# Attention and FFN with a Fourier stage: the scaled rows and the folds of the first two batches move from VectorE to GpSimd

## The chip, the core and the metric

The kernel runs on one core of a Trainium2 chip. Five engines of that core work side by side, each through its own list of instructions in a fixed order: TensorE (matmuls and transposes, PE in the profile), VectorE (DVE), ScalarE (ACT), GpSimd (POOL) and SyncE (SP), which starts most DMAs. They wait for one another only by semaphores. The metric is the device time of one execution in microseconds, as the median of several runs; lower is better.

## What is computed

```python
# per batch of 8; 12 heads, 448 rows, 64 columns per head
q_n, k_n = rmsnorm(q, g_q), rmsnorm(k, g_k)      # x / sqrt(mean(x*x) + 1e-6) * g
attn = softmax(q_n @ k_n.T / 8)
x = (attn @ v)                                   # heads side by side: [448, 768]
u = x + real(fft(fft(x, axis=rows), axis=columns))
un = (u - mean(u)) / sqrt(var(u) + 1e-6)
out = u + relu(un @ w_ch1) @ w_ch2               # [768, 3072] and [3072, 768]
```

All of it is float32. A matmul with fast operands is made from a rounded high part and a rest, so many values exist as a pair (copied by ScalarE, subtracted by VectorE).

## The kernel before

**Attention.** Heads are treated in pairs, six per batch. `norm_pair` (L250) normalises the rows of one pair: ScalarE squares the 1024 values per row (in batches 0 and 1; GpSimd does in later ones), VectorE sums them by 64 into the tile `ss`, GpSimd raises that to the power -0.5 (L265), and two multiplications (L267), one for queries and one for keys, scale the raw rows into the tile `qkn`. TensorE transposes `qkn` into `qk`, from which ScalarE and VectorE make the operands `QT` and `KD`/`rounded` of the scores. `softmax_pair` computes scores `S`, row minima `mn` (VectorE) and exponentials `P` (ScalarE). `value_pair` transposes `P` (`pt`, `rem`), multiplies with the values (`av`) and leaves a column block of `xT` per pair. In batches below `EARLY` = 2 the division by the row sums comes at the end of a pair (`divide_pair`): GpSimd copies the reciprocal sums wide (`rs`, L422), TensorE transposes them (`rt`), VectorE multiplies `xT` with them.

**Folds.** The Fourier transforms use the symmetry of rows and columns: `fold` (L551) adds and subtracts column blocks `p` and `p + 3` of `xT` (`eo`), then mirrored halves (`sd`), then mirrored quarters (`eo` again), and gathers three tiles EO[0], EO[1] and the total `tot`. There are three folds per batch; each has six steps of some 450 elements, and folds 1 and 2 also have some of 900. In batch 0, folds 0 and 1 run while the last two pairs are under way, fold 2 behind the last pair. `spectral` (L601) then multiplies EO with Fourier matrices (`y`, `Y`, `ab`), adds the result to the transposed rows (`u`), and normalises (`un`).

**FFN.** `ffn` (L973) runs 24 blocks `h` (18 matmuls each) and 36 blocks `o` (12 each). The attention of the next batch is mixed into it by `merge` (L1044). In batch 0 the weights also come in a 64-bit form and are converted by `convert` (L738): a DMA into `dbl`, two ScalarE steps, three VectorE steps on `mag`, one GpSimd addition (L763), then a rounded part (ScalarE) and a rest (VectorE). Some pieces (`mage`) are converted ahead, during the attention of batch 0.

**Order.** The program is written down in the order of these generators, and a scheduler then places the instructions of each engine by its own estimate of their times. So a change of an engine also changes where other instructions stand. All recorded operations share line L114 in the profile; they are told apart by their tiles.

## Time and profile before

| what | us |
|---|---|
| median of three runs (2165.72, 2174.75, 2173.51) | 2173.51 |
| span of the profiled execution, first to last instruction | 2158.8 |
| time of the profiled execution beside the span | not listed |
| TensorE busy, share of the span | 2085.6 (97%) |
| VectorE busy | 1551.6 (72%) |
| ScalarE busy | 1053.9 (49%) |
| GpSimd busy | 343.4 (16%) |

The attention of batch 0 stands alone and takes the first 177 us; then eight FFNs follow, with the attention of the next batch beside each of the first seven. Shares over the whole span say little about the first stages. In a timeline row stand the start, the length, the engine, line and operation, the tiles, the count, and in brackets the idle time just before with what ended it. The clock column is the granted TensorE clock, 1.00 being the full 2.4 GHz.

### The profile page before, as it was taken

What the parts mean: (1) busy time and instruction counts of PE and PEld (TensorE: products, weight loads), DVE (VectorE), ACT (ScalarE), POOL (GpSimd) and SP (SyncE); (2) the same over time, 40 slices, a digit from 0 to 9 for tenths busy, and PEclk for the clock granted to TensorE, in tenths of its full rate; (3) what the DMA queues carried; (4) which work ended last, traced back from release to release, by engine and by line L of the source; (5) the groups of instructions that cost most, each with busy time, mean ns of one, the idle gap of its engine ahead of it and who ended that gap; (6) DMA issues with size and microseconds to landing.
All of it is one profiled execution on the core that took longest, in us unless ns stands there. A gap on an engine that the chain in (4) does not pass through costs nothing.

```text
span 2158.8 us, 31384 instructions
## 1 busy us (share of the span) xinstructions
PE 2085.6 (97%) x11224; PEld 1858.1 (86%) x11224; DVE 1551.6 (72%) x3016; ACT 1053.9 (49%) x2258; POOL 343.4 (16%) x196
## 2 busy tenths in 40 slices
PE   7878999899999999999999999999999999999998
PEld 4557788788999999999999999999999989999998
DVE  7888788877885788758786688857787578754122
ACT  7967776455552555435552455425553355422100
POOL 4323334311110111001110011101110011000000
PEclk8977999999999999999999999999999999999999
DMA  5548877757555855667555666558556674458774
GB/s 172 181 125 272 257 249 255 243 200 214 170 167 182 238 180 168 175 206 225 161 176 177 215 197 176 171 190 239 171 165 188 204 209 142 150 175 251 234 248 150
DMA packets 294976, 424.79 MB, mean 197 GB/s; under 512 B 183283, under 2 KB 221156, under 8 KB 294820
## 3 DMA queue, kind: packets, MB, share of 16 engines
q1 hardware_dynamic: 290386, 420.67, 63.5%
q10 hardware_dynamic: 4434, 2.11, 0.4%
q8 instruction: 89, 1.46, 0.3%
q14 instruction: 67, 0.55, 0.1%
HBM read 362.53 MB, written 65.31 MB: 198 GB/s over the span
## 4 chain that ended last, share of the span: by engine, by line
PE 77%; DMA 3%; DVE 3%; ACT 1%; issue 1%; POOL 0%; DVEq 0%; SPq 0%; POOLq 0%; ACTq 0%
PE h L992 28%; PE o L1013 28%; PE S L382 5%; PE av L492 4%; PE pt L480 4%; DMA dbl<-w 2%; PE y L617 1%; PE qk L334 1%; PE oT L949 1%; PE x L649 1%; PE un L861 1%; PE av L497 1%; PE ab L694 1%; PE rem L437 1%; DMA u_dram<-u 1%
## 5 line engine op out<-in xcount | busy, mean ns | idle before, releaser
L1013 PE MATMUL o<-hs,w 128*128 128x448 f32 x3456 | 793.2, 372 | 2.9 <-DVE rounded L114 0.9
L992 PE MATMUL h<-unT,w 128*128 128x448 f32 x3456 | 784.0, 371 | 1.0 <-DVE hs L114 0.6
L1013 PEld LDWEIGHTS o<-hs,w 128*128 128x128 f32 x3456 | 638.4, 188 | 60.5 <-issue 3.8
L992 PEld LDWEIGHTS h<-unT,w 128*128 128x128 f32 x3456 | 639.8, 189 | 57.5 <-issue 4.1
L114 ACT ACTIVATE P<-S,mn 112x448 f32<-112x448 f32 x384 | 243.9, 637 | 196.9 <-DVE mn L114 188.1
L114 DVE TENSOR_REDUCE mn<-S 112x1 f32<-112x448 f32 x384 | 233.8, 617 | 33.0 <-PE S L382 30.3
L114 ACT ACTIVATE hs<-h 128x448 fp32r<-128x448 f32 x192 | 104.4, 544 | 304.5 <-PE h L992 302.9
L114 DVE SCALAR_TENSOR_TENSOR hs<-h,hs 128x448 fp32r<-128x448 f32 x192 | 119.3, 621 | 149.3 <-ACT hs L114 147.3
L114 DVE TENSOR_TENSOR acc<-o,acc 128x448 f32<-128x448 f32 (+1 forms) x240 | 147.0, 613 | 81.8 <-PE o L1013 79.1
L114 POOL TENSOR_TENSOR qkn<-raw 112x1024 f32<-112x1024 f32 x36 | 69.2, 1924 | 677.4 <-PE qk L334 391.5
L114 POOL TENSOR_TENSOR ss<-ss,nhalf 112x16 f32<-112x16 f32 x48 | 143.6, 2992 | 205.6 <-DVE ss L114 183.6
L382 PE MATMUL S<-KD,QT 128*112 128x448 f32 x384 | 152.8, 400 | 18.5 <-ACT KD L114 15.6
L114 ACT CAST T<-pt 128x448 fp32r<-128x448 f32 x216 | 112.9, 533 | 101.5 <-PE pt L480 97.9
L492 PE MATMUL av<-T,vhl 128*128 128x448 f32 x432 | 154.2, 385 | 0.8 <-DVE T L114 0.8
L114 DVE TENSOR_TENSOR T<-pt,T 128x448 fp32r<-128x448 f32 x216 | 131.7, 617 | 25.7 <-ACT T L114 24.7
L382 PE MATMUL S<-rounded,QT 128*112 128x448 f32 x384 | 143.7, 376 | 0.0
L114 DVE TENSOR_SCALAR P<-P,sm 112x448 f32<-112x448 f32 x288 | 122.7, 465 | 3.9
L480 PE MATMUL pt<-ident,P 112*128 112x112 f32 x864 | 122.1, 258 | 0.0
L480 PEld LDWEIGHTS pt<-ident,P 112*128 112x128 f32 x864 | 102.7, 140 | 15.8
L763 POOL TENSOR_TENSOR mag<-mag,dbl 128x512 uint32<-128x512 uint32 (+1 forms) x46 | 77.6, 1686 | 170.3 <-DVE mag L759 115.2
L114 POOL TENSOR_TENSOR rstd<-st,nhalf 112x1 f32<-112x1 f32 (+2 forms) x32 | 18.2, 570 | 505.7 <-DVE st L114 500.1
L382 PEld LDWEIGHTS S<-KD,QT 128*112 128x112 f32 x384 | 68.5, 179 | 29.4 <-ACT KD L114 18.7
(116 smaller groups left out, 2528.3 us busy)
## 6 DMA issues: line engine op xcount, KB each, us to landing
w<-w SPq DMA_DIRECT2D x192, 768.0 KB, 5.4
w<-w SPq DMA_DIRECT2D x288, 512.0 KB, 4.5
dbl<-w SPq DMA_DIRECT2D x28, 512.0 KB, 5.3
dbl<-w SPq DMA_DIRECT2D x18, 768.0 KB, 5.1
raw<-q SPq DMA_DIRECT2D x96, 112.0 KB, 3.9
raw<-k SPq DMA_DIRECT2D x96, 112.0 KB, 4.0
v<-v SPq DMA_DIRECT2D x96, 96.0 KB, 3.6
u_dram<-u SPq DMA_DIRECT2D x24, 336.0 KB, 3.1
```

Source lines behind the costliest of these rows:

```text
L114: ins = emit(*args, **kwargs)
L334: nc.tensor.transpose(pt[:, c * C : (c + 1) * C], qk[:, i, c].rearrange("t h d -> t (h d)"), ident[:C, :C],)
L382: ins = nc.tensor.matmul(s_, QT[:, h, cs], K[:, h], start=step == 0, stop=step == 1)
L437: nc.tensor.transpose(rem[:, c * C : (c + 1) * C], Pc[c][:, 384:512], ident[:C, :C])
L480: nc.tensor.transpose(pt[:, c * C : (c + 1) * C], Pc[c][:, 512 * h + j * 128 : 512 * h + (j + 1) * 128], ident[:C, :C],)
L492: nc.tensor.matmul(av[:, :S], lv, T[:, i], start=(j == 0 and i == 0), stop=False)
L497: nc.tensor.matmul(av[:, :S], lv, R[:, h], start=False, stop=True)
L617: nc.tensor.matmul(o, src[:, par, t0 : t0 + n], D1[:, ri, par, cols], start=i != 1, stop=i != 0,)
L649: nc.tensor.transpose(xp[:n, i * 128 : (i + 1) * 128], src[:, 3 * half + i], ident)
L763: behind(nc.gpsimd.tensor_tensor(out=bits, in0=bits, in1=low, op=ALU.add))
L992: pace(nc.tensor.matmul(o, w[:, a, c], unT[c][:, z], start=n == 0, stop=n == 17))
L1013: pace(nc.tensor.matmul(o, w[:, a, f], hs[4 * g + f][:, z], start=n == 0, stop=n == 11))
```

## The change

The two scalings of a pair run on GpSimd in batches 0 and 1. In `fold`, a local `add` and `sub` hide the functions of the same names: folds 0 and 1 of batch 0 and all three folds of batch 1 put their additions and subtractions on GpSimd. The `scalar_tensor_tensor` steps of a fold stay on VectorE, and fold 2 of batch 0 stays there whole. In later batches nothing changes.

```diff
--- before.py
+++ after.py
@@ -264,7 +264,7 @@
         )
         G.tensor_tensor(out=ss, in0=ss, in1=nhalf[:C], op=ALU.pow)
         for i in range(2):
-            V.tensor_tensor(
+            (G if b < EARLY else V).tensor_tensor(
                 out=qk[:, i].rearrange("t c h d -> t h c d"),
                 in0=raw[:, i],
                 in1=ss[:, 8 * i : 8 * i + 8]
@@ -561,6 +561,14 @@
                 halves[b] = wide(f"eo{b}_{p}")
             eo = halves[b][:, p % 2 * 900 : p % 2 * 900 + 900]
         eo = eo.rearrange("r (i t) -> r i t", i=2)
+        engine = G if b == 1 or (b == 0 and p < 2) else V
+
+        def sub(o, a, b_):
+            engine.tensor_tensor(out=o, in0=a, in1=b_, op=ALU.subtract)
+
+        def add(o, a, b_):
+            engine.tensor_tensor(out=o, in0=a, in1=b_, op=ALU.add)
+
         add(eo[:, 0, :449], xT[:, p, :449], xT[:, p + 3, :449])
         one, two = (4, 1) if p == 1 else (p, p + 3)
         sub(eo[:, 1, :449], xT[:, one, :449], xT[:, two, :449])
```

Names in the rows below end with the batch, the pair and a running number: `eo0_1` is fold 1 of batch 0, `qkn1_1` the scaled rows of pair 1 of batch 1, `mag_0_5_1` a conversion. Behind the change lines from 571 on are eight higher.

**The end of the attention of batch 0, on GpSimd.** Before, from the copy of the sums of pair 4 on:

```order
L114 COPY rs0_4_1233<-sums0_4_856 112x512
L763 TENSOR_TENSOR mage3_3_1074<-mage3_3_1074,dble3_3_1075 128x512
L763 TENSOR_TENSOR mage19_1167<-mage19_1167,dble19_1168 128x768
L114 TENSOR_TENSOR ss1_1_1344<-ss1_1_1344,nhalf_73 112x16
L114 COPY rs0_5_1386<-sums0_5_1053 112x512
L763 TENSOR_TENSOR mage4_1_1274<-mage4_1_1274,dble4_1_1275 128x512
```

With the change, the same piece of the list:

```order
L114 COPY rs0_4_1233<-sums0_4_856 112x512
L771 TENSOR_TENSOR mage19_1167<-mage19_1167,dble19_1168 128x768
L114 TENSOR_TENSOR eo0_1_1243<-xT0_295 128x449 x2
L114 TENSOR_TENSOR ss1_1_1344<-ss1_1_1344,nhalf_73 112x16
L114 TENSOR_TENSOR sd0_1_1242<-eo0_1_1243 128x2x225 x2
L771 TENSOR_TENSOR mage4_1_1274<-mage4_1_1274,dble4_1_1275 128x512
L114 TENSOR_TENSOR qkn1_1_1342<-raw1_1_1131,ss1_1_1344 112x2x4x64 x2
L114 TENSOR_TENSOR eo0_1_1243<-sd0_1_1242 128x4x113
L114 TENSOR_TENSOR eo0_1_1243<-sd0_1_1242 128x4x112
L114 TENSOR_TENSOR tot0_1250<-eo0_0_1046,eo0_1_1243 128x900
L114 COPY rs0_5_1386<-sums0_5_1053 112x512
```

Fold 1, its total and the scaling of pair 1 of batch 1 now stand between the power of that pair and the copy `rs0_5`, which stood right behind the power.

**The same place on VectorE.** Before, up to the first step of fold 2:

```order
L114 TENSOR_TENSOR qkn1_1_1342<-raw1_1_1131,ss1_1_1344 112x2x4x64 x2
L114 SCALAR_TENSOR_TENSOR eo0_0_1046<-eo0_1_1243,eo0_0_1046 128x900
L755 TENSOR_SCALAR mage4_1_1274<-mage4_1_1274 128x512
L114 TENSOR_REDUCE mn1_0_0_1262<-S1_0_0_1_1264 112x1
L759 SCALAR_TENSOR_TENSOR mage4_1_1274<-dble4_1_1275,mage4_1_1274 128x512
L114 TENSOR_REDUCE mn1_0_1_1312<-S1_0_1_0_1313 112x1
L765 TENSOR_TENSOR w1e4_1_1273<-mage4_1_1274,w1e4_1_1273 128x512
L114 TENSOR_REDUCE mn1_0_1_1312<-S1_0_1_1_1314 112x1
L114 TENSOR_TENSOR xT0_295<-rt0_5_1388,xT0_295 128x448
L114 TENSOR_REDUCE mn1_0_2_1371<-S1_0_2_0_1372 112x1
L114 TENSOR_TENSOR QT1_1_1434<-qk1_1_0_1436,QT1_1_1434 64x448 x2
L114 TENSOR_TENSOR eo0_2_1396<-xT0_295 128x449 x2
```

With the change:

```order
L114 TENSOR_REDUCE mn1_0_1_1312<-S1_0_1_0_1313 112x1
L773 TENSOR_TENSOR w1e4_1_1273<-mage4_1_1274,w1e4_1_1273 128x512
L114 TENSOR_REDUCE mn1_0_1_1312<-S1_0_1_1_1314 112x1
L114 TENSOR_REDUCE mn1_0_2_1371<-S1_0_2_0_1372 112x1
L114 TENSOR_REDUCE mn1_0_2_1371<-S1_0_2_1_1373 112x1
L114 SCALAR_TENSOR_TENSOR eo0_0_1046<-eo0_1_1243,eo0_0_1046 128x900
L114 TENSOR_TENSOR QT1_1_1434<-qk1_1_0_1436,QT1_1_1434 64x448 x2
L114 TENSOR_TENSOR xT0_295<-rt0_5_1388,xT0_295 128x448
L114 TENSOR_TENSOR eo0_2_1396<-xT0_295 128x449 x2
L114 TENSOR_TENSOR sd0_2_1395<-eo0_2_1396 128x2x225 x2
```

The scalings are gone, the step on EO[0] (`eo0_0` from `eo0_1`) stands behind the row minima and in front of `QT1_1`, the division of the last pair and fold 2.

**The end of the attention of batch 1, on GpSimd.** Before:

```order
L114 COPY rs1_5_3946<-sums1_5_3281 112x512
L763 TENSOR_TENSOR mag_0_22_3932<-mag_0_22_3932,dbl_0_22_3933 128x768
L763 TENSOR_TENSOR mag_0_23_3981<-mag_0_23_3981,dbl_0_23_3982 128x768
L763 TENSOR_TENSOR mag_0_5_1_4034<-mag_0_5_1_4034,dbl_0_5_1_4035 128x512
L763 TENSOR_TENSOR mag_0_5_2_4071<-mag_0_5_2_4071,dbl_0_5_2_4072 128x512
L763 TENSOR_TENSOR mag_0_5_3_4116<-mag_0_5_3_4116,dbl_0_5_3_4117 128x512
```

With the change:

```order
L114 COPY rs1_5_3946<-sums1_5_3281 112x512
L771 TENSOR_TENSOR mag_0_22_3932<-mag_0_22_3932,dbl_0_22_3933 128x768
L771 TENSOR_TENSOR mag_0_23_3981<-mag_0_23_3981,dbl_0_23_3982 128x768
L114 TENSOR_TENSOR eo1_2_3956<-xT1_1764 128x449 x2
L771 TENSOR_TENSOR mag_0_5_1_4034<-mag_0_5_1_4034,dbl_0_5_1_4035 128x512
L114 TENSOR_TENSOR sd1_2_3955<-eo1_2_3956 128x2x225 x2
L771 TENSOR_TENSOR mag_0_5_2_4071<-mag_0_5_2_4071,dbl_0_5_2_4072 128x512
L114 TENSOR_TENSOR eo1_2_3956<-sd1_2_3955 128x4x113
L114 TENSOR_TENSOR eo1_2_3956<-sd1_2_3955 128x4x112
L114 TENSOR_TENSOR eo1_1_3794<-eo1_1_3794,eo1_2_3956 128x900
L114 TENSOR_TENSOR tot1_3801<-tot1_3801,eo1_2_3956 128x900
L771 TENSOR_TENSOR mag_0_5_3_4116<-mag_0_5_3_4116,dbl_0_5_3_4117 128x512
```

The eight steps of fold 2 stand between the conversions, the last four in front of `mag_0_5_3`.

**The same place on TensorE**, where the spectral matmuls `y1` read the folded tiles. Before:

```order
L992 MATMUL h0_21_4093<-unT0_4_1717,w2_0_21_3905 128x448 x3
L992 MATMUL h0_21_4093<-unT0_5_1725,w2_0_21_3905 128x448 x3
L617 MATMUL y1_0_0_4009<-D1_76,eo1_0_3639 113x2x65
L617 MATMUL y1_0_1_4046<-D1_76,eo1_0_3639 112x2x65
L617 MATMUL y1_1_0_4083<-D1_76,eo1_0_3639 113x2x65
L617 MATMUL y1_1_1_4128<-D1_76,eo1_0_3639 112x2x65
L617 MATMUL y1_0_0_4009<-D1_76,eo1_1_3794 113x2x65
```

With the change:

```order
L1000 MATMUL h0_22_4151<-unT0_4_1717,w1_0_22_3931 128x448 x3
L1000 MATMUL h0_22_4151<-unT0_5_1725,w1_0_22_3931 128x448 x3
L625 MATMUL y1_0_0_4009<-D1_76,eo1_0_3639 113x2x65
L625 MATMUL y1_0_1_4046<-D1_76,eo1_0_3639 112x2x65
L625 MATMUL y1_1_0_4083<-D1_76,eo1_0_3639 113x2x65
L625 MATMUL y1_1_1_4128<-D1_76,eo1_0_3639 112x2x65
L1000 MATMUL h0_23_4244<-unT0_0_1685,w2_0_23_3980 128x448 x3
L1000 MATMUL h0_23_4244<-unT0_1_1693,w2_0_23_3980 128x448 x3
L1000 MATMUL h0_23_4244<-unT0_2_1701,w2_0_23_3980 128x448 x3
L1000 MATMUL h0_23_4244<-unT0_3_1709,w2_0_23_3980 128x448 x3
L1000 MATMUL h0_23_4244<-unT0_4_1717,w2_0_23_3980 128x448 x2
L625 MATMUL y1_0_0_4009<-D1_76,eo1_1_3794 113x2x65
```

Block 22 of the FFN now stands in front of the first `y1`, and most of block 23 behind the first four.

## Rows read from the trace of the kernel before

**Rows 1.** Busy us by stage: stretch; PE, PEld, DVE, ACT, POOL; clock; DMA

```profile
25.00:120.00 95.00, 77.06 (x373) 51.28 (x373) 85.20 (x145) 91.03 (x202) 37.67 (x21) 0.93 0.56 167
120.00:148.00 28.00, 18.40 (x67) 12.38 (x65) 26.11 (x48) 17.74 (x38) 6.66 (x3) 0.73 0.50 158
148.00:177.00 29.00, 16.72 (x86) 14.05 (x85) 22.06 (x50) 18.67 (x32) 8.61 (x7) 0.62 0.57 198
177.00:425.00 248.00, 239.15 (x1175) 198.72 (x1176) 203.57 (x329) 170.11 (x333) 94.94 (x55) 0.98 0.78 254
425.00:473.00 48.00, 39.64 (x220) 35.80 (x218) 33.26 (x71) 21.25 (x42) 8.59 (x8) 0.94 0.65 230
...
570.00:2158.80 1588.80, 1581.16 (x8722) 1449.42 (x8720) 1087.55 (x2189) 668.42 (x1467) 164.32 (x86) 1.00 0.63 190
```

**Rows 2.** Waits of ScalarE from 120 to 150 us: total us, times, longest

```profile
ACT P L114 <- DVE mn L114: 8.9, 3, 5.2
```

**Rows 3.** Groups of VectorE by form, first 500 us: busy us, mean ns | idle before

```profile
L114 DVE TENSOR_REDUCE mn<-S 112x1 f32<-112x448 f32 x107 | 64.1, 616 | 4.9 <-PE S L382 4.4
L114 DVE TENSOR_TENSOR qkn<-raw,ss 112x512 f32<-112x512 f32 x30 | 23.2, 811 | 4.5 <-POOL ss L114 4.4
```

**Rows 4.** Groups of GpSimd by form, whole span

```profile
L114 POOL TENSOR_TENSOR qkn<-raw 112x1024 f32<-112x1024 f32 x36 | 69.2, 1924 | 677.4 <-PE qk L334 391.5 <-DMA w<-w 162.2 <-DVE hs L114 102.9
L763 POOL TENSOR_TENSOR mag<-mag,dbl 128x512 uint32<-128x512 uint32 x28 | 41.1, 1468 | 91.5 <-DVE mag L759 61.6 <-ACT P L114 5.8 <-ACT hs L114 5.1
...
L114 POOL COPY rs<-sums 112x512 f32<-112x512 f32 x12 | 11.1, 922 | 19.4 <-PE av L456 19.4
```

**Rows 5.** Timeline of VectorE and TensorE, first pair

```profile
11.68 1.29 DVE L114 TENSOR_TENSOR qkn<-raw,ss 112x512 f32<-112x512 f32 x2 [3.11 <-POOL ss L114]
12.51 1.11 PE L334 MATMUL qk<-ident,qkn 112*128 112x112 f32 x8 [1.02 <-DVE qkn L114]
```

**Rows 6.** Timeline of VectorE and GpSimd, end of the attention of batch 0

```profile
119.86 0.62 DVE L114 TENSOR_TENSOR xT<-rt,xT 128x448 f32<-128x448 f32 x1
...
126.11 2.90 POOL L114 TENSOR_TENSOR ss<-ss,nhalf 112x16 f32<-112x16 f32 x1 [6.31 <-DVE ss L114]
...
138.24 1.26 DVE L114 TENSOR_TENSOR QT<-qk,QT 64x448 fp32r<-64x448 f32 x2
139.53 1.16 DVE L114 TENSOR_TENSOR eo<-xT 128x449 f32<-128x449 f32 x2
```

**Rows 7.** Timeline of VectorE and GpSimd, two places where both work

```profile
369.63 2.72 POOL L114 TENSOR_TENSOR qkn<-raw 112x1024 f32<-112x1024 f32 x1 [1.94 <-PE qk L334]
370.51 2.25 DVE L755 TENSOR_SCALAR mag<-mag 128x768 uint32<-128x768 uint32 x1
...
391.91 1.32 POOL L763 TENSOR_TENSOR mag<-mag,dbl 128x512 uint32<-128x512 uint32 x1 [3.59 <-DVE mag L759]
392.13 2.12 DVE L114 TENSOR_TENSOR sd<-eo 128x450 f32<-128x450 f32 x2
```

**Rows 8.** Timeline of GpSimd, VectorE and TensorE, end of the FFN of batch 0

```profile
418.08 2.38 POOL L763 TENSOR_TENSOR mag<-mag,dbl 128x768 uint32<-128x768 uint32 x1 [4.71 <-DVE mag L759]
421.74 3.82 PE L992 MATMUL h<-unT,w 128*128 128x448 f32 x18
429.79 3.67 PE L617 MATMUL y<-D,eo 128*113 128x130 f32 x16 [4.23 <-DVE eo L114]
430.57 1.08 DVE L114 TENSOR_TENSOR tot<-tot,eo 128x900 f32<-128x900 f32 x1
...
436.60 2.49 PE L992 MATMUL h<-unT,w 128*128 128x448 f32 x11
...
470.72 0.94 PE L861 MATMUL un<-ident,un 112*128 112x112 f32 x4 [3.75 <-ACT un L114]
```

**Rows 9.** Timeline of GpSimd and TensorE, pair 4 of batch 1

```profile
265.17 2.90 POOL L114 TENSOR_TENSOR ss<-ss,nhalf 112x16 f32<-112x16 f32 x1 [4.09 <-DVE ss L114]
...
271.71 0.57 PE L334 MATMUL qk<-ident,qkn 112*128 112x112 f32 x4 [2.31 <-DVE qkn L114]
```

## The prediction

> **What bounds the kernel now.** I read the busy time by stage first [rows 1], because the change ends with batch 1 and an average over the span would hide where that is. From 570 us on TensorE is busy for 1581 of 1589 us: nothing done on VectorE or GpSimd can shorten that, and from about there on the order of every engine is the same before and after. What can move lies in the first 570 us, in five stretches; they end at 177 and 473 us because the first FFN matmul of batches 0 and 1 starts there.
> - Until 25 us: the start. The normalisation of the first pair is one chain with nothing else to do; TensorE waits for it [rows 5].
> - 25 to 120 us (attention of batch 0): ScalarE is busy for 91.0 of 95 us, VectorE for 85.2, TensorE for 77.1. ScalarE sets the pace, with 4.0 us idle.
> - 120 to 148 us (end of that attention, folds): VectorE is busy for 26.1 of 28 us; ScalarE waits for its row minima for 8.9 us [rows 1, 2]. VectorE sets the pace.
> - 148 to 177 us (spectral part of batch 0): no engine is full; it is a chain of short steps. The change has no instruction here.
> - 177 to 473 us (FFN of batch 0 with the attention of batch 1 beside it): TensorE is busy for 239.2 of 248 us and then for 39.6 of 48 us. So 8.8 and 8.4 us are all that can be won. Three waits hold 10.3 us of them: 2.31 us for a scaled pair [rows 9], 4.23 us for the last fold of batch 1, 3.75 us for its last normalised tile [rows 8].
>
> **What leaves VectorE.** Two scalings (L267) of each of 12 pairs: 24 instructions; two take 1.29 us where nothing disturbs them [rows 5], so 15.5 us. Of the folds 34: in batch 0 twelve of some 450 elements and one of 900, in batch 1 eighteen and three. Two of 450 take 1.16 us [rows 6], one of 900 takes 1.08 us [rows 8]: 13.0 + 1.1 and 10.4 + 3.2, hence 8.0 us (12 x 0.58 + 1.08) before 148 us and 13.7 us (18 x 0.58 + 3 x 1.08) after 177 us. With 16 scalings before 148 us (10.3 us), VectorE loses 18.3 us there and 18.8 us later, 37 us in all. With disturbed ones counted the mean of a scaling is higher, 0.81 us [rows 3].
>
> **What GpSimd gets.** Before does not run an f32 operation with two different inputs there. The nearest rows: a square of 1024 elements at 1.92 us and an integer addition of 512 at 1.47 us, strided and partly disturbed [rows 4]. By elements that is 0.85 to 1.29 us for 450, 0.96 to 1.47 us for 512, 1.7 to 2.6 us for 900. I take 1.05, 1.2 and 2.1, between the two, since a fold has two inputs like the addition but plain rows like the square. So GpSimd gets 24 x 1.2 + 30 x 1.05 + 4 x 2.1 = 69 us, for 37 us taken from VectorE. It has room (busy 95 of 248 us in the fullest long stretch), so what counts is the length of its chains. The moved steps start no DMA; the raw rows that the scalings free lie in two buffers, and the next load into one of them belongs to the pair after next, some 18 us later, so 1 us more holds nothing. The Trainium skill, GPSIMD Engine Reference, section "Elementwise — side-by-side cycle accounting", has 4497 ns on GpSimd against 2293 ns on VectorE for an addition of 2048 f32. By that a fold step would be about 0.99 us and a scaling 1.12 us (estimates), and the forecast below would be about 1 us lower. The rows of before neither confirm nor deny it.
>
> **The sum, stretch by stretch.**
> (a) Start. Nothing hides the first pair: behind the power, two scalings take 2.4 us and not 1.3. Only the second is late by all of it, and keys and queries are both needed for a score: +1.0 us (bounds +0.6 to +1.6).
> (b) 25 to 120 us. VectorE is relieved of 7 pairs and most of fold 0, but ScalarE has only 4.0 us to lose. The later scalings (about 1 us each) are covered by the exponentials of the pair before. I take half: -2.0 us (-4 to 0; if ScalarE comes to wait for a late pair, its cover is gone and this is 0).
> (c) 120 to 148 us. Here the change puts fold 1 on GpSimd in front of the copy rs0_5, which the last division and so fold 2 need. I count from T, the end of the xT of pair 4 at 119.86 + 0.62 = 120.48 us [rows 6]. Before, fold 2 starts at 139.53, T + 19.05. After, on GpSimd: start T + 0.4; two sums 2.1; the power, when its input is there (T + 2.7), 2.9; two 2.1; one conversion 1.47; two scalings 2.4; two 2.1; the total 2.1: T + 15.8; rs 0.92 [rows 4]: T + 16.7. On VectorE the scalar_tensor_tensor on EO[0] now waits for that total, and behind it stand QT of the next pair, xT and fold 2: 15.9 + 1.1 + 1.3 + 0.6 and a ScalarE copy of one column, T + 19.2. That is +0.1; a row minimum (0.62 us [rows 3]) no longer stands within fold 2: -0.5 us (bounds -3 with the short prices, +2.5 with the long ones, and more if the steps wait, see the first rival).
> (d) 148 to 177 us: 0.
> (e) 177 to 425 us. The wait of 2.31 us ends at 271.71; the power before it ends at 265.17 + 2.90 = 268.07 [rows 9], and two scalings right behind it on GpSimd end at 270.5: -1.2 us. Small losses elsewhere leave -1.0 us (-4 to +3). The 18.8 us off VectorE are worth nothing more here, since TensorE hides them.
> (f) 425 to 473 us. TensorE has now 18 more matmuls (h0_22, 3.8 us as the 18 of h0_21) in front of the first y, and 14 of h0_23 behind its first four. GpSimd: the conversion that starts at 418.08 ends at 420.5; two sums 422.6; conversion 424.1; two 426.2; conversion 427.7; two 429.8; then 1.1 us on VectorE: 430.9. TensorE is through with h0_22 at 421.74 + 3.82 + 3.82 = 429.4, so the wait is about 1.6 us instead of 4.23: -2.6 us [rows 8]. EO[1] and the total follow at 431.9 and 434.0, behind 14 matmuls that last until 435. Against that, y ends 3.5 us later than 436.6 and less FFN work is left to cover the spectral chain. Batch 0 took 29 us for the whole of it, y included [rows 1], some 21 us behind y; here TensorE still has about 20 us. So I leave the last wait nearly as it is, with 1.6 us of transposes moved into it, and take 1.2 us off the whole for a chain that may show: -3.0 us (-6 to +5).
> Sum: +1.0 - 2.0 - 0.5 - 1.0 - 3.0 = -5.5 us, on a span of 2158.8 us: 2153.3 us. The execution that was profiled has no time of its own beside the span; the median of the three runs lies 14.7 us above it, and I keep those 14.7 us: 2168.0 us, 0.25% under 2173.5.
>
> **Rivals.**
> 1. Slower: the two engines hold each other up. The rows show it: the two VectorE subtractions at 392.13 took 2.12 us and not 1.16, with a GpSimd addition running; a tensor_scalar took 2.25 us beside a GpSimd square, which itself took 2.72 instead of 1.92 [rows 4, 7]. Put +0.8 us on each of the 9 moved steps in (c) and the 6 in (f) before y, with the long prices: (c) +7.2 + 2.5, (f) +4.8 + 1.5, (b) lost +2, (e) +1, 19.0 us more, so 2187.0 us. It decides from where a pair of fold steps takes over 2.8 us on GpSimd (5.5 us over 15 steps). Against it: in these stretches VectorE mostly reads PSUM (minima, hs, acc), and those rows show no such stretch. The Trainium skill states it as a rule in SBUF — State Buffer, section "Who interferes with whom": GpSimd and a VectorE instruction with two inputs in SBUF share a port, and whichever starts second waits for the whole of the first. The trace agrees in the rows just named (2.12 and 2.25 us).
> 2. Clearly faster: VectorE is the bound all the way to 148 us. Then (b) gives all 4.0 us, (c) most of the 8.9 us that ScalarE waited (7), (e) 2 and (f) 6, less 0.6 for (a): -18.4 us, 2155.1 us. For it: 26.1 of 28 us busy. Against it: the GpSimd chain of (c) is as long as the VectorE one that it replaces.
> 3. Nothing moves: ScalarE and TensorE keep their pace and the waits only change their names: 2174 us. For it: TensorE 99% busy after 570 us, and 4% idle in the long stretch before it.
>
> **How the numbers follow.** A difference of 0.5% (10.9 us) is about what a measurement can tell from none. Forecast 0.50, first rival 0.13, second 0.15, third 0.22. Under 2162.6 us: 0.13 of the second and 0.08 of the forecast's own spread, 0.21. Over 2184.4 us: 0.08 of the first and 0.03 of the others, 0.11. The rest, 0.68, is no difference. Range 2157 to 2182 us: the bounds of (b), (c) and (f) do not all fall on one side at once; alone the forecast's own is 2161 to 2176.
>
> **What would show it.** (a) the first qk 1 us or less later behind its power; (b) ScalarE idle under 3 us from 25 us to the last xT; (c) GpSimd's total of fold 1 ending about 16 us behind the xT of pair 4, and VectorE idle before the scalar_tensor_tensor on EO[0]; (e) no wait of 2 us for qkn; (f) a wait of 1 to 2.5 us before y, and the first h of batch 1 at 465 to 471 us. The forecast is wrong if the first h of batch 0 moves by over 5 us from 177, if fold pairs on GpSimd take over 2.8 us, or if y waits over 5 us.

## The result

The changed kernel takes 2186.2 us (median of 5 runs, 2182.7 to 2191.1) against 2167.0 us of the kernel before (5 runs): a ratio of 1.0085, with a 95% interval of 1.0067 to 1.0103, so 18 us slower. The forecast was 2168.0 us; the first rival, in which the two engines hold each other up, had 2187.0 us. That the two numbers meet is partly luck: the rival stood on a starting time of 2173.5 us, 6.5 us above the 2167.0 us measured now, and as a change it was 13.5 us, against 18 to 20 measured.

The profiled execution has a span of 2189.3 us, 30.5 us more than that of before. Eleven of these are spread between executions: the run with the span of 2189.3 us took 2191.13 us, 1.8 us more than the span; so the profiled execution of before (2158.8 us) lies some 6 us under its median and this one 5 us over its own. The loss is read from the stages. The busy time by stage of the changed kernel, in stretches that end at about the same events as those of before [rows 1], columns as there (stretch, length; PE, PEld, DVE, ACT, POOL; clock; DMA share and GB/s):

```profile
25.00:128.00 103.00, 79.68 (x364) 53.13 (x365) 82.07 (x133) 92.40 (x205) 57.14 (x38) 0.88 0.55 164
128.00:157.00 29.00, 18.86 (x70) 11.39 (x69) 19.51 (x31) 17.56 (x38) 16.29 (x12) 0.74 0.39 118
...
189.60:450.00 260.40, 243.00 (x1188) 201.77 (x1189) 207.89 (x307) 172.71 (x334) 127.10 (x81) 0.97 0.76 246
...
600.00:2189.30 1589.30, 1579.39 (x8714) 1449.11 (x8712) 1084.97 (x2185) 667.20 (x1465) 164.09 (x86) 1.00 0.63 190
```

The first FFN matmul of batch 0 starts at 189.60 us (177.06 before), that of batch 1 at 497.60 (472.96): 12.5 us are lost before the first, 12.1 us between them. The other 5.9 of the 30.5 us lie behind 497.60 us, where nothing was moved; a second profile of the same kernel has 12.1, 12.6 and 0.8 us for the three, so those 5.9 us are scatter of a single execution. VectorE's share of the first two stretches has fallen, as intended: it is idle for 21 of 103 us and 9.5 of 29 us. But nobody uses that: ScalarE is idle for 10.6 us of the first (4.0 us in 25 to 120 us before), and TensorE for 17.4 of 260 us of the third (8.8 of 248 before). From 600 us on TensorE is busy for 1579 of 1589 us, as before. Over the whole span TensorE's busy time rose from 2085.6 to 2094.1 us with the same 11224 instructions, while its mean granted clock fell from 0.983 to 0.976; in the first stretch it is 0.88, against 0.93 in 25 to 120 us before [rows 1].

Over the whole span VectorE's busy time went from 1551.6 to 1543.6 us. The instructions that left it had 37 us, so some 29 us came back in instructions that stayed. GpSimd's went from 343.4 to 415.5 us. Which instructions were stretched shows in VectorE's groups by form in the first 500 us of the changed kernel (count, then busy us and mean ns, then idle time before):

```profile
L114 DVE TENSOR_REDUCE mn<-S 112x1 f32<-112x448 f32 x100 | 60.1, 616 | 16.1 <-PE S L382 15.5 <-ACT P L114 0.2
...
L759 DVE TENSOR_SCALAR mag<-mag 128x512 f32<-128x512 f32 x28 | 20.6, 737 | 19.6 <-ACT mag L757 19.4
...
L767 DVE SCALAR_TENSOR_TENSOR mag<-dbl,mag 128x768 uint32<-128x768 uint32 x18 | 20.1, 1119 | 0.1
```

and the same two conversion steps, two of the eight forms that the conversions of whole pieces take, in the kernel before, with the first additions of the folds:

```profile
L759 DVE SCALAR_TENSOR_TENSOR mag<-dbl,mag 128x768 uint32<-128x768 uint32 x18 | 17.2, 957 | 0.3
L751 DVE TENSOR_SCALAR mag<-mag 128x512 f32<-128x512 f32 x28 | 16.0, 573 | 14.8 <-ACT mag L749 14.4
...
L114 DVE TENSOR_TENSOR eo<-xT 128x449 f32<-128x449 f32 x12 | 7.7, 685 | 0.3 <-ACT xT L114 0.3
```

The row minima, which read PSUM, keep their 616 ns [rows 3]. The two conversion steps shown, which read SBUF alone, went from 957 to 1119 and from 573 to 737 ns. Of the eight such forms six rose and two fell; all conversions of weights together, the ones ahead included, took 28 of the 29 us (165.4 before, 194.0 with the change).

The end of the FFN of batch 0, to be read beside [rows 8]: VectorE, ScalarE, GpSimd and TensorE from the last division of batch 1 (xT) to the first spectral matmul (y), in order of time (start, duration):

```profile
440.40 0.62 DVE L114 TENSOR_TENSOR xT<-rt,xT 128x448 f32<-128x448 f32 x1
...
443.13 0.66 ACT L757 ACTIVATE mag<-dbl 128x512 f32<-128x512 f32 x1 [4.03 <-DMA dbl<-w]
...
444.97 0.19 ACT L114 COPY xT<-xT 128x1 f32<-128x1 f32 x1
445.24 2.69 POOL L114 TENSOR_TENSOR eo<-xT 128x449 f32<-128x449 f32 x2 [3.03 <-ACT xT L114]
...
454.04 2.52 POOL L114 TENSOR_TENSOR eo<-sd 128x452 f32<-128x452 f32 x2
...
456.76 2.98 DVE L114 SCALAR_TENSOR_TENSOR eo<-eo,eo 128x900 f32<-128x900 f32 x1
...
459.88 2.05 PE L625 MATMUL y<-D,eo 128*113 128x130 f32 x8 [8.34 <-DVE eo L114]
```

The division ends at 441.02, the fold on GpSimd starts 4.2 us later, takes 11.3 us for its first six steps (445.24 to 456.56), and the scalar_tensor_tensor on VectorE behind it takes 2.98 us instead of the 1.08 us of a step of this size before. TensorE waits 8.34 us (4.23 before).

### The profile page after: what moved, and what is told of

Same layout as the page of the kernel before. It is cut to its first block, busy times and chain, and to the rows that moved or that the text cites. A ratio compares the mean times of both kernels' runs of the same rounds, so it can differ in the third digit from the quotient of the medians.

```text
span 2189.3 us, 31465 instructions
## 1 busy us (share of the span) xinstructions
PE 2094.1 (96%) x11224; PEld 1865.6 (85%) x11224; DVE 1543.6 (71%) x2958; ACT 1054.5 (48%) x2258; POOL 415.5 (19%) x254
## 4 chain that ended last, share of the span: by engine, by line
PE 80%; ACT 6%; DVE 5%; DMA 5%; POOL 2%; issue 2%; SPq 1%; DVEq 0%; ACTq 0%; POOLq 0%
PE h L1000 29%; PE o L1021 28%; PE S L382 6%; PE av L492 4%; PE pt L480 4%; DMA dbl<-w 3%; PE y L625 2%; PE qk L334 1%; ACT P L114 1%; POOL mag L771 1%; PE av L456 1%; DMA u_dram<-u 1%; PE oT L957 1%; PE un L869 1%; PE av L497 1%
## 5 line engine op out<-in xcount | busy, mean ns | idle before, releaser
L114 DVE TENSOR_TENSOR T<-pt,T 128x448 fp32r<-128x448 f32 x216 | 131.8, 617 | 24.3 <-ACT T L114 23.2
L114 POOL TENSOR_TENSOR rstd<-st,nhalf 112x1 f32<-112x1 f32 (+2 forms) x32 | 19.9, 623 | 514.6 <-DVE st L114 506.7
```

Source lines behind the costliest of these rows:

```text
L114: ins = emit(*args, **kwargs)
```

## Experiments

Three theories. **A**: GpSimd and VectorE hold each other up where both read SBUF. **B**: steps are longer on GpSimd, and so are the chains through it. **C**: the scheduler orders all engines' instructions anew when the estimates of some change, and the other order loses the time. Every ratio is to runs of the kernel before on the same chip, 4 to 12 runs each; us are the ratio less one, times 2165.

| kernel | order of instructions | ratio, 95% interval | us |
|---|---|---|---|
| scalings of batch 0 moved | its own | 1.0039, 1.0025 to 1.0053 | +8.4 |
| scalings of batch 1 moved | its own | 1.0031, 1.0021 to 1.0042 | +6.7 |
| folds of batch 0 moved | its own | 1.0071, 1.0058 to 1.0084 | +15.4 |
| folds of batch 1 moved | its own | 1.0026, 1.0015 to 1.0037 | +5.6 |
| nothing moved | that of the changed kernel | 1.0130, 1.0115 to 1.0145 | +28.1 |
| all moved | that of before | 1.0104, 1.0088 to 1.0120 | +22.5 |
| all scalings moved | that of before | 1.0011, 0.9997 to 1.0025 | +2.4 |
| folds of batch 0 moved | that of before | 1.0010, 0.9999 to 1.0021 | +2.2 |
| folds of batch 1 moved | that of before | 1.0046, 1.0033 to 1.0059 | +10.0 |
| all folds moved | that of before | 1.0058, 1.0045 to 1.0071 | +12.6 |
| scalings and folds of batch 0 moved | that of before | 1.0045, 1.0028 to 1.0062 | +9.7 |
| short scalings on VectorE | that of before | 0.9984, 0.9973 to 0.9995 | -3.5 |
| short scalings on GpSimd | that of before | 0.9991, 0.9980 to 1.0001 | -1.9 |
| 58 unread twins on GpSimd | that of before | 1.0149, 1.0134 to 1.0164 | +32.3 |
| 62 unread fills on GpSimd | that of before | 1.0039, 1.0025 to 1.0053 | +8.4 |
| changed, column copy earlier | that of changed but for one | 1.0103, 1.0089 to 1.0117 | +22.3 |
| changed kernel again | its own | 1.0092, 1.0079 to 1.0106 | +19.9 |

**The four parts alone**, each in the order that the scheduler makes for it:

```
-            (G if b < EARLY else V).tensor_tensor(        # b == 0, b == 1, or V
-        engine = G if b == 1 or (b == 0 and p < 2) else V # one of the two, or V
```

> Only the 12 scalings of batch 0 on GpSimd, everything else as in the kernel before. The whole change came out about 19 us slower; between the traces 7.8 us of it are lost before the last division of pair 4 of batch 0, where all scalings of batch 0 but few folds lie. Theory A (GpSimd and VectorE hold each other up: operations with both inputs in SBUF, and tensor_scalars, run longer on VectorE while GpSimd works, and the moved steps run longer too): +6 to +9 us over the kernel before, and VectorE's conversions of weights (lines 751 to 765) in the first 120 us have means at least 10% higher than before, while minima from PSUM keep 616 ns. Theory B (only the longer chain of a pair counts, 2.0 us for two scalings instead of 1.3): +1 to +5 us with VectorE's conversions as before. Theory C (the scheduler's other order of instructions loses the time): no relation to these durations.

> Only the 12 scalings of batch 1 on GpSimd. Pair 0 and a part of pair 1 of batch 1 are normalised before 177 us, the rest beside the FFN of batch 0, where TensorE has work in hand. Theory A: +1 to +4 us, with the loss around the last division of batch 0 and little in 177 to 425 us, since stretched conversions are hidden behind TensorE there. Theory B: -1 to +2 us. Theory C: anything up to +6 us.

> Only folds 0 and 1 of batch 0 on GpSimd (12 additions of some 450 elements and one of 900). Theory A: +3 to +6 us, all of it between 120 us and the first FFN matmul of batch 0: the chain of fold 1, with pairs of 2.2 us and more, ends later in front of the copy for the last division. Theory B: the same chain with undisturbed steps (1.9 to 2.05 us a pair) makes it +1 to +3 us. The first FFN matmul of batch 0 tells the place (177.1 us before, 189.6 with the whole change).

> Only the folds of batch 1 on GpSimd (18 additions of some 450 elements, 3 of 900). With the whole change the FFN of batch 0 takes 12.1 us more (308.0 instead of 295.9). Theory A: +8 to +13 us, almost all of it at the end of that FFN, where the first matmul of the spectral part waits 7 to 9 us for the last fold (4.23 us before), with pairs of 2.4 to 2.7 us on GpSimd and scalar_tensor_tensor on EO[0] at 2 to 3 us (1.1 to 1.3 before). Theory B: pairs stay at 1.9 to 2.1 us and the sum is +3 to +6 us. My prediction had -3 us for this place.

Measured (table): together 36 us, twice the loss of the whole. (The expectations of later runs quote differences of medians, 34 us in sum.) The scalings of batch 0 came out in theory A's range, those of batch 1 (6.7) over every range. The folds of batch 1 (5.6) lie under A's range and inside B's, those of batch 0 far over both: there the first FFN matmul of batch 0 starts at 185.45 us (+8.4), and the FFN of batch 0, in which this kernel moves nothing, takes another 8 us more, in waits of TensorE that sum to 24.9 us from 185 to 490 us (16.9 us before). That speaks for C.

**Engines and order apart.** In these and most of the following kernels the order of every engine is taken from another build, instruction by instruction:

```
+    for n in scheduled:            # instruction names, in the other build's order
+        two = made[n]
+        one, last[two.engine] = last.get(two.engine), two
+        if one is not None:        # same engine: order alone, no semaphore
+            tc.add_manual_dep(two, one.name, ...)
```

> The engines of the kernel before (all scalings and folds on VectorE), but every engine issues its instructions in the order of the changed kernel; the 58 moved instructions are left free to stand where the scheduler puts them on VectorE. The parts alone cost 7.4, 6.2, 13.8 and 6.2 us, together 34, while the whole costs 19 to 21, and with only the folds of batch 0 moved 8 us are lost in the FFN of batch 0, where that kernel moves nothing; so the order of the rest is a suspect. Theory C (the order loses the time): +12 to +21 us over the kernel before. Theories A and B (the engines hold each other up; longer chains on GpSimd): 0 to +4 us, since nothing runs on GpSimd that did not before.

> The engines of the changed kernel (scalings and folds on GpSimd), but every engine issues its instructions in the order of the kernel before; on GpSimd the moved instructions stand where they stood in the order of the whole program. Theory C (the order loses the time): -6 to +4 us against the kernel before, that is most of the loss is gone. Theory A (the engines hold each other up): +12 to +25 us. Theory B (only longer chains on GpSimd): +5 to +12 us, with VectorE's conversions of weights at their means of before (line 755 at 478 ns for 512 elements, line 759 at 957 ns for 768).

Neither theory alone predicts both. The new order with the old engines costs 28 us, over every range, but it was made for a VectorE without the 58 instructions, which were put back wherever the scheduler chose. The new engines in the old order cost 22.5 us, inside A's range alone: so the loss does not need the new order, and the scheduler's own order (18 to 20 us) is hardly better than the old one. For the whole change C falls as the only cause. For single parts it holds: the folds of batch 0 cost 2.2 us in the order of before (below) and 15.4 in their own.

**Unread work beside VectorE**, in the order of before:

```
+            twins.append(G.tensor_tensor(out=spare[...], in0=raw[:, i], in1=ss[...], op=ALU.mult))
```

> The kernel before, with its order of instructions on every engine kept, and 58 more instructions on GpSimd that nobody reads: beside each scaling a copy of it on GpSimd into a spare tile, and at the start of each of the five folds as many additions of the same sizes (from the attention output, into the spare tile). VectorE keeps all its work and waits for none of the new instructions; they can cost only through what the two engines share, and through GpSimd's queue. Theory A (they hold each other up): +8 to +25 us, and in the first 500 us VectorE's operations with both inputs in SBUF have means 10 to 30% above before (line 759: 722 and 957 ns), while those fed from PSUM keep theirs (minima 616 ns, acc 615 ns). Theories B and C: -2 to +4 us, all means as before.

Nobody waits for a twin, VectorE's instructions are the same 3016, and the kernel is 32 us slower, more than the change itself and more than theory A's +8 to +25: each twin stands beside its original, so the two engines probably meet more often than in the changed kernel. VectorE's busy time rises from 1551.6 to 1588.8 us, by 37 us for 83 us more of GpSimd (426.7 against 343.4). The groups of VectorE in its first 500 us:

```profile
L114 DVE TENSOR_REDUCE mn<-S 112x1 f32<-112x448 f32 x98 | 58.8, 616 | 2.6 <-PE S L392 2.0
L114 DVE TENSOR_TENSOR qkn<-raw,ss 112x512 f32<-112x512 f32 x28 | 35.9, 1319 | 3.1 <-POOL ss L114 3.1
...
L779 DVE SCALAR_TENSOR_TENSOR mag<-dbl,mag 128x768 uint32<-128x768 uint32 x18 | 18.2, 1014 | 0.3
...
L114 DVE TENSOR_TENSOR eo<-xT 128x449 f32<-128x449 f32 x12 | 13.9, 1202 | 0.3 <-ACT xT L114 0.3
```

Minima from PSUM stay at 616 ns; the scalings went from 811 [rows 3] to 1319, the first additions of the folds from 685 to 1202 ns, the two-input conversion from 957 to 1014 only.

**The disputed cost by itself.**

```
+        for _ in range(2 * N if v else 0): v_op(v, vo, x, p)   # VectorE, 16 of a kind
+        for _ in range(N if g else 0): g_op(g, go, x)          # GpSimd, 8 of a kind
```

> A kernel that computes nothing of the reference (it writes zeros): 20 stretches, in each of which VectorE runs 16 operations of one kind, GpSimd 8 of one kind, or both at the same time. Theory A: VectorE's addition of 450 with both inputs in SBUF takes 0.56 to 0.6 us alone and 0.9 us or more as a mean beside GpSimd's additions, whose own mean goes from about 1.0 alone to 1.4 us or more; a VectorE addition with one input in PSUM, a minimum over PSUM and a sum over one SBUF input keep their durations; a tensor_scalar from SBUF is stretched too. If GpSimd only writes (a fill), the addition with two SBUF inputs is not stretched but the tensor_scalar is. Theories B and C: every duration beside the other engine within 10% of that alone. For the prices: additions of 450 at 1.05 and of 900 at 2.1 us on GpSimd, a scaling of 512 at 1.2 us, as in my forecast.

Names tell what ran beside what ("two": two SBUF inputs; "one": a tensor_scalar; "psum": one input in PSUM). On both sides an addition of 900 opens each stretch, so the means with and without a partner hold it alike:

```profile
L35 DVE TENSOR_TENSOR two_beside_add<-x 128x450 f32<-128x450 f32 x16 | 18.3, 1144 | 0.5
...
L41 DVE TENSOR_SCALAR one_beside_add<-x 128x450 f32<-128x450 f32 x16 | 14.6, 911 | 0.6
...
L41 DVE TENSOR_SCALAR one_beside_fill<-x 128x450 f32<-128x450 f32 x16 | 12.9, 807 | 0.5
L35 DVE TENSOR_TENSOR two_beside_fill<-x 128x450 f32<-128x450 f32 x16 | 11.8, 738 | 0.6
L35 DVE TENSOR_TENSOR two_beside_None<-x 128x450 f32<-128x450 f32 x16 | 11.8, 738 | 0.6
L50 POOL TENSOR_TENSOR add_along_two<-x 128x450 f32<-128x450 f32 x8 | 11.2, 1397 | 0.6
...
L37 DVE TENSOR_TENSOR psum_beside_add<-p,x 128x450 f32<-128x450 f32 x16 | 10.0, 627 | 0.6
...
L39 DVE TENSOR_REDUCE min_beside_add<-p 128x1 f32<-128x450 f32 x16 | 10.0, 626 | 0.6
...
L50 POOL TENSOR_TENSOR add_along_None<-x 128x450 f32<-128x450 f32 x8 | 9.1, 1133 | 0.6
...
L41 DVE TENSOR_SCALAR one_beside_None<-x 128x450 f32<-128x450 f32 x16 | 8.1, 505 | 0.5
```

By medians the VectorE addition of two SBUF inputs takes 628 ns alone and 1439 beside GpSimd's additions; beside GpSimd's fills it keeps its 628. The tensor_scalar takes 396 ns alone, 1205 beside additions and 999 beside fills; its row means (505, 911, 807) also hold the first operation of each stretch and the last ones, which run when GpSimd is through. With one input in PSUM (627 ns without a partner too) or in a minimum over PSUM nothing changes (626 ns both). GpSimd's own addition goes from 1133 to 1397 ns; the one of 900 takes 2078 alone. Theory A holds in each of its cases; only the sizes miss a little (628 ns alone where 560 to 600 were expected, 1397 where 1.4 us or more were). In the stream one VectorE addition and one of GpSimd get done in about 1.45 us (eight of GpSimd's in 11.72 us), while VectorE alone does two in 1.26 us: in such a stream, moving every other addition is a loss by itself. The Trainium skill, SBUF — State Buffer, section "Who interferes with whom", says just this: VectorE with two SBUF inputs meets GpSimd's reads and not its writes, a tensor_scalar may contend as well, and an instruction with at most one SBUF input, outside the two-port modes that a tensor_scalar can enter, meets neither. The trace agrees in the rows above.

**Reads or queue?** The twins again, as fills that hold GpSimd's queue for as long:

```
-                twins.append(G.tensor_tensor(out=spare[...], in0=raw[:, i], in1=ss[...], op=ALU.mult))
+                twins.append(G.tensor_copy(spare[:C, :1], ss[:, :1]))
+                twins.append(G.memset(spare, 0.0))
```

> As the kernel with 58 unread twins on GpSimd in the order of before, which cost 31.4 us, but each twin is now a fill of 900 columns of the spare tile (0.85 us alone in the small kernel, behind a copy of one column that ties it to the same place; two fills for the widest), so GpSimd's queue is held for about as long and SBUF is written but hardly read. Theory A as the small kernel has it (two-input operations of VectorE are held up by GpSimd's reads alone, tensor_scalars by its writes too): +3 to +12 us, with the two-input operations of the first 500 us (lines 759 and 765 of before) at their means of before and tensor_scalars (lines 751, 755) stretched. If it is GpSimd's queue that costs (powers, copies and conversions standing behind the twins): +20 us or more.

GpSimd is busy for 245.4 us of the first 500 (246.6 with the twins), and the cost is 8.4 us instead of 32.3. VectorE's groups there:

```profile
L114 DVE TENSOR_TENSOR qkn<-raw,ss 112x512 f32<-112x512 f32 x28 | 22.3, 835 | 4.5 <-POOL ss L114 4.4
...
L762 DVE TENSOR_SCALAR mag<-mag 128x512 f32<-128x512 f32 x28 | 19.2, 684 | 14.2 <-ACT mag L760 14.1
...
L770 DVE SCALAR_TENSOR_TENSOR mag<-dbl,mag 128x768 uint32<-128x768 uint32 x18 | 17.2, 955 | 0.3
...
L114 DVE TENSOR_TENSOR eo<-xT 128x449 f32<-128x449 f32 x12 | 7.8, 686 | 0.3 <-ACT xT L114 0.3
```

Scalings take 835, folds 686 and the two-input conversion 955 ns, near the 811, 685 and 957 ns of before; only the tensor_scalar is clearly longer, at 684 ns (573 before). So about 24 of the 32 us came from GpSimd's reads, and the queue and the writes have the rest.

**What the relief is worth**, in the order of before:

```
+            few = 1 if moved and b < EARLY else D
+                out=qk[:, i]...[:, :, :, :few], in0=raw[:, i, :, :, :few], ...
```

> The kernel before and its order, but in the first two batches each scaling covers one of 64 columns, so the other columns of queries and keys stay the unscaled squares: VectorE is relieved of some 13 us and nothing is added anywhere. It tells what the relief of VectorE is worth by itself, with no price for it. My forecast took ScalarE and TensorE for the bound and gave the relief of 37 us some 4 us: by that -2 to -6 us here (1.1 us of it from the shorter first pair). If VectorE is the bound before 177 us, -8 to -14 us.

> As the kernel that scales one of 64 columns, with these short scalings on GpSimd behind the power: VectorE is relieved of the scalings, GpSimd holds nothing for long, and the chain of a pair no longer goes back to VectorE. Theory A (only long operations that read SBUF on both sides cost): within 3 us of the kernel with the short scalings on VectorE, so -2 to -8 us against the kernel before. Theory B (it is GpSimd's place in the chain that costs): +3 us or more over that kernel.

Taking 13 us off VectorE for nothing gains 3.5 us (1.1 to 5.8): VectorE is not the bound before 177 us, as forecast. With the short scalings on GpSimd it is 1.9 us; the two intervals overlap, so GpSimd's place in the chain of a pair costs next to nothing here. Theory B falls for the scalings.

**The parts in the order of before.**

```
-        engine = G if moved and (b == 1 or (b == 0 and p < 2)) else V
+        engine = G if moved and b == 0 and p < 2 else V     # folds of batch 0; so the others
```

> Only folds 0 and 1 of batch 0 on GpSimd, and every engine's order kept as in the kernel before. With the scheduler's own order this part cost 13.8 us, of which 8.3 us lay in the FFN of batch 0, where nothing is moved. Theory A with C (what the move itself costs lies before the first FFN matmul; the rest is the scheduler's other order): +4 to +8 us, the first FFN matmul of batch 0 at 181 to 186 us and its FFN within 3 us of the 298.9 us of before. Without C: +11 to +15 us and an FFN that is 6 us or more longer.

> Only the 24 scalings of both batches on GpSimd, every engine's order kept as in the kernel before. Scalings and folds together cost 22.5 us in this order. Theory A (held up by each other): +7 to +13 us, and the first FFN matmul of batch 0 4 to 8 us later. Theory B alone (each pair is longer by 0.8 us on GpSimd, covered but for the first): 0 to +4 us.

> Only the folds of batch 1 on GpSimd, every engine's order kept as in the kernel before. In this order all moves together cost 22.5 us, the scalings alone 3.4, the folds of batch 0 alone 2.6. If the costs add, 16 us are left for this part: +13 to +18 us, all in the FFN of batch 0. If they don't add (theory D: single delays fit into the slack of the fixed order, together they exceed it): +2 to +6 us.

> Both batches' folds on GpSimd, scalings on VectorE, order kept as in the kernel before. If costs add: 2.6 us and the cost of the folds of batch 1 alone, within 3 us. Theory D: more than the sum of the two by 4 us or more.

> All scalings and the folds of batch 0 on GpSimd, those of batch 1 on VectorE, order kept as in the kernel before. If costs add: 3.4 and 2.6, so +4 to +8 us. Theory D: +10 us or more, with the first FFN matmul of batch 0 10 us later, as with all moves in this order (187.7 against 177.1 us), where each part alone gave 2.1 and 5.4.

The scalings cost 2.4 us, less than A had; the folds of batch 0 cost 2.2, less than the 4 to 8 expected, with the first FFN matmul at 182.51 us and their FFN at 300.8 us, both in the expected ranges (298.9 us before, 307.2 in their own order, each up to the end of the transposes of un). The folds of batch 1 cost 10.0 us, between the two ranges. The folds add up (2.2 + 10.0 against 12.6). Scalings and folds of batch 0 together cost 9.7 us against 4.6 in sum; the intervals reach down to 6.1, so their meeting is likely, not certain. The first FFN matmul starts at 187.85 us, 10.8 later than before, as theory D had it; the 9.7 us lie just under D's 10. The likely place is GpSimd's queue in front of the last division (the copies rs are what a division needs), here with both moved, with TensorE's and VectorE's waits behind it:

```profile
115.37 5.14 POOL L114 TENSOR_TENSOR eo<-sd 128x452 f32<-128x452 f32 x2
120.45 0.61 POOL L114 COPY rs<-sums 112x512 f32<-112x512 f32 x1
121.12 1.01 PE L425 MATMUL rt<-ident,rs 112*128 112x112 f32 x4 [4.79 <-POOL rs L114]
...
140.41 2.89 POOL L114 TENSOR_TENSOR qkn<-raw,ss 112x512 f32<-112x512 f32 x2
140.48 1.92 DVE L114 SCALAR_TENSOR_TENSOR eo<-eo,eo 128x900 f32<-128x900 f32 x1 [5.88 <-POOL tot L114]
143.25 0.80 POOL L114 COPY rs<-sums 112x512 f32<-112x512 f32 x1
```

A pair of fold 0 takes 5.14 us, and the copy of pair 4 stands behind it; later a pair of scalings takes 2.89 us right behind the total of fold 1, with the copy of pair 5 behind that. That copy ends at 144.05 us; with the folds alone at 136.58, with the scalings alone at 134.72, before at 132.88. TensorE's wait of 4.79 us for the copy of pair 4 is 0.98 us with the folds alone and none with the scalings alone; VectorE's wait of 5.88 us for the total is in neither.

The folds of batch 1 are the dearest part. GpSimd, VectorE and TensorE at the end of the FFN of batch 0, with these alone moved:

```profile
433.18 1.10 DVE L114 SCALAR_TENSOR_TENSOR eo<-eo,eo 128x900 f32<-128x900 f32 x1 [0.95 <-POOL eo L114]
433.23 3.00 POOL L114 TENSOR_TENSOR eo<-eo,eo 128x900 f32<-128x900 f32 x1
...
434.33 1.14 PE L625 MATMUL y<-D,eo 128*113 128x130 f32 x8 [3.96 <-DVE eo L114]
...
436.18 2.27 POOL L114 TENSOR_TENSOR tot<-tot,eo 128x900 f32<-128x900 f32 x1
```

y waits no longer than before (3.96 us), but behind the first 8 matmuls it needs EO[1] and the total, which take 3.00 and 2.27 us on GpSimd where VectorE took 1.08 each; y starts 4.5 us later than before, and the h behind it 7.1 us later (443.66 against 436.60). Of the 3.00 us, 2.08 are GpSimd's own price (B); the rest fits contention (A), since in the small kernel the same step beside a VectorE addition of 900 takes 2.99 us.

**One instruction of the order.** In the changed kernel ScalarE's copy of one column (0.19 us, at 444.97) stands behind a conversion that waits 4.03 us for its transfer, and the fold starts behind it; before, it followed the division at once.

```
+        wanted.remove(early_one.name)
+        wanted.insert(wanted.index(scalar[at - 3]), early_one.name)
```

> The changed kernel and its order, but one instruction moved: ScalarE's copy of one column of the attention output, behind the last division of batch 1 (0.19 us), stands three places earlier, in front of three conversion steps of weights. In the changed kernel it starts at 444.97 us, 3.9 us behind the end of the division (441.02), because the first of those steps waits 4.03 us for its transfer; the last fold on GpSimd starts behind it at 445.24. In the kernel before it followed 0.03 us after the division. Theory C (the other order holds a part of the loss): the fold starts within 1 us of the division, the wait of the first spectral matmul falls from 8.3 to 4 to 6 us, and the time by 2 to 4 us. Theory A alone: the folds then meet more of VectorE's work, and the time stays within 1 us.

> The changed kernel once more, beside the one with the moved column copy, so that the two are timed on the same chip: 1.0085 of the kernel before as measured (18 us over it), within 3 us.

```profile
438.12 0.62 DVE L115 TENSOR_TENSOR xT<-rt,xT 128x448 f32<-128x448 f32 x1
...
439.89 1.92 POOL L115 TENSOR_TENSOR eo<-xT 128x449 f32<-128x449 f32 x2
...
443.75 1.82 POOL L772 TENSOR_TENSOR mag<-mag,dbl 128x512 uint32<-128x512 uint32 x1 [1.94 <-DVE mag L768]
...
445.53 2.45 POOL L115 TENSOR_TENSOR sd<-eo 128x450 f32<-128x450 f32 x2
...
456.44 2.08 PE L626 MATMUL y<-D,eo 128*113 128x130 f32 x8 [7.19 <-DVE eo L115]
```

The fold now starts 1.15 us behind the division instead of 4.2. But its second pair (445.53) stands in GpSimd's queue behind a weight conversion that waits for its data; y still waits 7.19 us, and the time is the same (1.0103 and 1.0092, intervals overlapping). Theory C's gain of 2 to 4 us is refuted: the next wait took it.

No experiment gave a version that is faster than the kernel before and computes the same.

## Why the prediction was wrong

The mechanism that the runs support is the first rival's, which had a chance of 0.13: the small kernel, the twins and the fills show that the two engines hold each other up. That its number was met is luck. It put its 19.0 us on (b) +2, (c) +9.7 and (e) and (f) +7.3; against the forecast the spans show +9.0 on (b), +4.9 on (c), +16.1 on (e) and (f), and +5.9 behind all of them.

Two terms of the forecast's sum failed: (e) and (f), forecast at -4.0 us and measured at +12.1, a miss large enough to turn the sign alone, and (b), forecast at -2.0 and measured at +7.0. Behind both is the same gap: the sum put the price on VectorE's remaining work at nothing, and likewise the price of the scheduler's other order. By the forecast's own steps, from the trace of the changed kernel:

- **Unit prices.** Right for GpSimd alone: 1.05, 1.2 and 2.1 us forecast, 0.98 to 1.13 (a reversed and a plain addition), 1.04 and 2.08 in the small kernel. In the changed kernel the means are 1.22 for a scaling, 1.11 to 1.32 for a fold step, and 2.1 to 2.9 for 900 elements. The estimates from the Trainium skill, GPSIMD Engine Reference, section "Elementwise — side-by-side cycle accounting" (0.99 and 1.12 us), fit as well. What was missing is a price on the other engine: VectorE's remaining work grew by some 29 us. (In the list of what leaves VectorE, the 13.0 us for twelve steps of some 450 elements should be 7.0; the 8.0 us beside it, which the sum uses, are right.)
- **(a)** +1.0 forecast, +0.94 measured (qk at 13.45 instead of 12.51 [rows 5]). Most of that is luck: the power in front of it already ended 0.62 us later (12.27 against 11.65), because the first load landed later. Behind the power the first qk is 0.3 us later, the end of the second transposes 0.8 us:

```profile
12.35 2.04 POOL L114 TENSOR_TENSOR qkn<-raw,ss 112x512 f32<-112x512 f32 x2
...
13.45 0.60 PE L334 MATMUL qk<-ident,qkn 112*128 112x112 f32 x4 [2.46 <-POOL qkn L114]
```

- **(b)** -2.0 forecast. This step failed. The xT of pair 4 ends at 128.39 us instead of 120.48: +7.9 us, 7.0 of them here. That relief of VectorE is worth about 3 us was right (the short scalings). Wrong was the cover: I had the later scalings hidden behind the exponentials of the pair before. In the views of waits (before until 177 us, changed until 190) VectorE's wait for scores grew from 3.4 to 13.2 us, ScalarE's wait for minima from 12.7 to 17.1: the pair's chain itself is late, with VectorE idle beside it. The powers on GpSimd date it: that of pair 1 starts 1.0 us later than before (20.55), that of pair 3 4.4 us (52.42), that of pair 0 of batch 1 7.0 us (111.21). The condition for this was in the prediction ("if ScalarE comes to wait for a late pair") at the price of a gain lost, 0, not of a loss. Two runs size it: with all scalings moved in the order of before, that xT ends 1.7 us later than before (122.17), and with those of batch 0 moved in the scheduler's own order 6.4 us later (126.84):

```profile
121.54 0.63 DVE L114 TENSOR_TENSOR xT<-rt,xT 128x448 f32<-128x448 f32 x1
...
126.26 0.58 DVE L114 TENSOR_TENSOR xT<-rt,xT 128x448 f32<-128x448 f32 x1
```

So the move itself accounts for some 1.7 us of it, and in the second of these runs the scheduler's other order for some 4.7; why that order is slower here stays open.
- **(c)** -0.5 forecast, +4.4 measured (the first y matmul 28.7 us behind that xT, 24.3 before; 27.1 in the second profile, so +2.8). The chain of fold 1 came out as counted: the total ends 16.6 us behind the xT, 15.8 forecast. But the division did not wait for it:

```profile
127.77 0.62 DVE L114 TENSOR_TENSOR xT<-rt,xT 128x448 f32<-128x448 f32 x1
...
128.76 2.09 POOL L114 TENSOR_TENSOR eo<-xT 128x449 f32<-128x449 f32 x2 [2.56 <-ACT xT L114]
...
142.84 2.12 POOL L114 TENSOR_TENSOR tot<-eo,eo 128x900 f32<-128x900 f32 x1
...
145.66 0.61 POOL L114 COPY rs<-sums 112x512 f32<-112x512 f32 x1 [0.70 <-PE av L456]
...
151.45 0.62 DVE L114 TENSOR_TENSOR xT<-rt,xT 128x448 f32<-128x448 f32 x1 [1.69 <-ACT xT L114]
...
152.33 1.16 DVE L114 TENSOR_TENSOR eo<-xT 128x449 f32<-128x449 f32 x2 [0.26 <-ACT xT L114]
```

The copy rs is done at 146.27 and the division starts at 151.45, when ScalarE has the last attention values; fold 2 starts 23.9 us behind T, not 19.2. I had followed GpSimd and VectorE and not the values of pair 5, which had become late as well.
- **(d)** 0 forecast, +0.3 measured (32.5 us from the first y matmul to the first h).
- **(e), (f)** -4.0 forecast, +12.1 measured. The wait of 2.31 us for a scaled pair is gone, as forecast, and TensorE loses more in many small waits. The y wait is 8.34 us, not 1.6: the fold started 3.0 us later behind its xT than forecast (4.2 instead of 1.2, the column copy), its six steps took 11.3 instead of 9.3 us, and the scalar_tensor_tensor 2.98 instead of 1.1. That wait grew by 4.1 us over before, so it holds 4.1 of the 12.1; the rest is spread over many small waits.
- **The threshold of the first rival** (a pair over 2.8 us) was too high: pairs of 2.5 to 2.7 us were enough at this place, since VectorE's own steps paid too, which the threshold left out. Against that rival I had said that VectorE mostly reads PSUM there. It does for minima, hs and acc; it does not for the 46 weight pieces of four steps each, and one of the two places that showed it [rows 7] was such a step (a tensor_scalar, which the sentence from the Trainium skill on two inputs does not cover, though the small kernel shows it stretched); the other was a fold beside a conversion on GpSimd.
- **The bridge from span to time.** The 14.7 us between the profiled span and the median were taken as constant. Runs with both show 1.8 us; the rest was the spread of single executions. This constant and the high starting time are what made the rival's number meet the measured one.

Open stays how the loss splits between stretched steps, GpSimd's queue and longer chains, and the scheduler's order, both in the changed kernel and in its 22.5 us in the fixed order: the twins price contention with VectorE unrelieved, not in the changed kernel itself.

## What to carry to other kernels

An instruction on GpSimd that reads SBUF is not free for VectorE: before moving work there, count what VectorE still reads from SBUF at that time, and price both sides with the other busy. Work whose VectorE neighbours read PSUM did not stretch them (626 and 627 ns with and without GpSimd's additions in the small kernel); work beside conversions or other SBUF-to-SBUF steps is paid for on both engines. And where a scheduler sets the order, time each move also with the old order kept, or the price of the new order is taken for that of the move.

## What the runs showed of the hardware that was not expected

- The two engines do not wait for one another by semaphores alone, as the start of this text has it: they hold each other up where no semaphore is between them. Unread GpSimd work placed beside VectorE's own cost nearly half its time there: 83 us of it made VectorE busy for 37 us more, with its instructions unchanged. In the changed kernel it was some 29 us for 72 us more on GpSimd.
- The loss is on both sides: side by side, VectorE's addition of 450 goes from 628 to 1439 ns and GpSimd's from 1133 to 1397 ns; an addition of 900 on GpSimd that meets one on VectorE takes 2.99 us instead of 2.08.
- On GpSimd the addition with one input read backwards was not slower than the plain one (982 against 1133 ns for 450 elements).
